# One quarter of x transposed by TensorE and three quarters by DMA, rows of Q padding and output weights loaded elsewhere, and the plan drawn from 24 candidates

## The chip, the cores and the metric

The kernel runs on one core of a Trainium2 chip. The metric is device time in microseconds (us). The kernel before took 361.9 us, the median of three runs (361.76 to 362.11). A difference below 0.2% (0.7 us) cannot be told from no change here.

## The reference: what is computed

One block of multi-head attention with S = 2048 rows, model width D = 448, 16 heads of 28 columns each, all in bf16:

```python
qkv = (x @ wqkv).reshape(B, S, 3, H, Dh)          # x: 1 x 2048 x 448, wqkv: 448 x 1344
q, k, v = ...                                     # each B, H, S, Dh
scores = jnp.einsum("bhqd,bhkd->bhqk", q, k) * (Dh ** -0.5)
p = _softmax(scores, axis=-1)
o = jnp.einsum("bhqk,bhkd->bhqd", p, v)
out = o.transpose(0, 2, 1, 3).reshape(B, S, D) @ wo
```

## The kernel before, in words

**Tiling.** Heads are taken in 4 groups of 4 (G, HG), each head padded from 28 to 32 rows, so that a group fills 128 partitions. The queries are cut into 4 chunks of 512 (QW, NQC), the keys into 16 blocks of 128 (NKT). One pair of group and chunk is a *set*; there are 16 sets. Within a set every head has 16 steps, one for each block of keys: a score matmul of 128 keys by 512 queries (line 730), the exponential, and a matmul of the result with V that adds into the set's accumulator `o` (line 1073). That makes 1024 steps in all.

**Two paths for the exponential.** ScalarE takes two steps at once: one `activation` with Exp over 128x1024 values of PSUM tile `a0` or `a1` into `pt` (line 928). VectorE takes single steps: it turns the scores of PSUM bank `d0`, `d1` or `m` into int16 bit patterns `I` that read as bf16 powers of two (line 943), and adds two shifted copies `J` (line 1014); for some chains one copy is made by GpSimd's fill (line 979) and an accumulating DMA (line 990). 358 instructions of ScalarE take 716 steps and 308 of VectorE the other 308.

**What comes first.** Before the first scores can be computed, the kernel needs:

- x with its columns on the partitions (`XT`, four blocks b of 512 rows). x arrives in `xs[b]` as eight loads of half a block, four from SP's DMA queue and four from ScalarE's (lines 145 to 149). TensorE transposes each block against an identity, two banks of eight transposes for each block (`xt_job`, line 621); ScalarE copies one bank to `XT` (line 629) and VectorE the other (line 627). The contraction of 448 is cut into 4 pieces of CK = 112.
- the weights of group 0 for K and Q (`WG`, loads of 232-byte rows, lines 151 and 152), and later all three weights (`WRAW`, line 136).
- K of all four blocks for group 0 (`k_first`, projections at line 298), its squares on ScalarE (`sq`, line 324), column sums by TensorE (line 409), their maximum on VectorE (`kp`, line 414) and a root: the softmax's bound is the product of a query's norm and the largest norm of a key. This bound rides along as extra rows of Q.
- Q of set 0 (`z`, line 457) and its bound (`su`, line 496).

**Q's padding rows.** For each chunk c, half k and buffer z there is a tile `QP[c][k][z]`. VectorE clears all 16 of them (line 194), then SP issues 16 small DMAs of a constant `offs` into some of their rows (line 198), then four DMAs bring set 0's rows of `z` into them (`rows_first`, line 661), then two bring `su` (line 502). Until these have landed, a score of set 0 is made of two matmuls, with `z` and with `su`; afterwards of one, with `QP` (`emit_s`, line 730). The text below calls the first form *narrow*.

```python
terms = [QP[c][i % 2][g % 2]] if w else [qtt[0], held["su0"]]
```

**GpSimd's opening** clears the V tiles (lines 209, 210) and the output weights `WO` (line 216), and issues 16 DMAs that load `WO` head by head (line 219).

**Order of the work.** `tc.manual_schedule()` is on: every engine runs its instructions in the order in which the program emits them. The middle of the program is a planner. It keeps a clock for each engine (`free`), a table of events with the time at which it believes them to happen (`evt`), and PSUM banks with the time at which they come free (`res`); a job (`add`) has an engine, an assumed duration, the events it needs and a priority. The planner moves the engine with the earliest clock, picks what that engine does next (`pick_pe`, `pick_act`, `pick_dve`, `pick_pool`, `pick_sp`), and emits it. Its times only set the order: on the chip each instruction waits for its real inputs. Loads are given to it as fixed due times:

```python
for n, t in (("x", 0), 4.9), (("G", 1), 6.9), (("G", 0), 6.9), (("x", 1), 6.2), (("x", 2), 8.0), (("x", 3), 9.3), \
        (("W", 2), 10.9), (("W", 0), 12.0), (("W", 1), 13.2):
    evt[n] = (t, "DMA")
```

**End of a set.** VectorE copies `o` to `o_sb` (line 1100); SP gathers the denominators, scatters their reciprocals to DRAM and spreads them (lines 1105, 1114, 1120); GpSimd multiplies (line 1123) into `xs` or `OTL`. Output projections (`oproj_job`) and stores (line 600) follow once all four groups of a chunk are done; the last chunk has a hand-written end (lines 1293 to 1350).

Of the kernel before, what the change touches and what calls it, by code (L numbers as in the profile page):

```python
# [16 lines left out]
LAT = 0.2  # L17
# [20 lines left out]

@with_exitstack
def kernel(  # L40
# [16 lines left out]
    CK = D // CC  # L57
# [11 lines left out]
    NXB = NKT // XB  # L69
    SHIFT = (0, 43, 85)  # L70
# [20 lines left out]
    NSET = G * NQC  # L91
    GH = 2
# [6 lines left out]
    out_perm = out2.rearrange("(p t) d -> p t d", t=NKT)  # L99
# [7 lines left out]
    XT = [[big.tile([CK, CC // 2, QW], BF16, name=f"XT{b}_{k}") for k in range(2)] for b in range(NXB)]  # L107
# [15 lines left out]
    xs = [big.tile([P, XB, D], BF16, name=f"xs{b}") for b in range(NXB)]  # L123
    QP = [[[big.tile([P, QW], BF16, name=f"QP{c}_{k}_{z}") for z in range(2)] for k in range(2)] for c in range(NQC)]
    OTL = [big.tile([P, QW], BF16, name=f"OTL{c}") for c in range(NQC)]

    def otile(g, c):
        if g < G - 1:
            return xs[c][:].rearrange("p t d -> p (t d)")[:, g * QW:(g + 1) * QW]
        return OTL[c][:]  # L130

    wq3 = wqkv.rearrange("(cc p) n -> p cc n", p=CK)
    x3 = x2.rearrange("(p t) c -> p t c", t=NKT)

    def load_w(t, eng):
        eng.dma_start(out=WRAW[t][:, :, 0:D], in_=wq3[:, :, t * D:(t + 1) * D])

    def load_x(b, eng, k=0, n=1):
        w = XB // n
        eng.dma_start(out=xs[b][:, k * w:(k + 1) * w, :], in_=x3[:, b * XB + k * w:b * XB + (k + 1) * w, :])  # L140

    def load_w0(t, eng):
        eng.dma_start(out=WG[t], in_=wq3[:, :, t * D:t * D + HG * Dh + WPAD])
# [33 lines left out]
    offs = wk.tile([P, 2 * QW], BF16, name="pt", bufs=NPT)[0:2, 0:QW]  # L177
# [12 lines left out]
    nc.vector.memset(offs, OFFS)  # L190
    for c in range(NQC):
        for k in range(2):
            for z in range(2):
                nc.vector.memset(QP[c][k][z][:], 0.0)
    for z in range(2):
        for c in range(NQC):
            for k in range(2):
                nc.sync.dma_start(out=QP[c][k][z][HP * k + Dh + NQC - 1 - c:P:2 * HP, :], in_=offs)
# [4 lines left out]
    for t in range(3):  # L203
        nc.gpsimd.memset(WRAW[t][:, :, D:D + WPAD], 0.0)

# [21 lines left out]
    def pair_tile(tg):  # L227
        return psum.tile([P, 2 * QW], F32, name=tg, tag=tg, bufs=1)

    def bank_tile(tg):  # L230
        return psum.tile([P, QW], F32, name=tg, tag=tg, bufs=1)


    free = {"PE": 0.0, "ACT": 0.0, "DVE": 0.0, "SP": 0.0, "POOL": 26.0}
    port = {"DVE": 0.0, "POOL": 0.0}
    evt = {}
    res = {"a0": 0.0, "a1": 0.0, "d0": 0.0, "d1": 0.0, "o": 0.0, "m": 0.0}
    ops = {"PE": [], "ACT": [], "DVE": [], "SP": [], "POOL": []}
    cnt = {"step": 0, "half": 0}
    held = {}  # L240
    cur = {"c_end": 0.0, "s": 0, "u": 0, "o": None, "oset": 0, "pv": 0, "half": 0, "o_open": False}
    parts = {}

    def add(eng, dur, emit, **k):
        op = Op(eng, dur, emit, **k)
        ops[eng].append(op)
        return op

    def ready(op):
        if cnt["step"] < op.gate or (op.acq == "m" and op.gives[0][0] == "O" and left() < OLAST):  # L250
            return None
        if op.acq == "m" and op.pri > 5 and ("KN0", NQC - 1) not in evt:
            return None
        r = 0.0
        for n in op.need:
            if n not in evt:
                return None
            t, e = evt[n]
            r = max(r, t + (0.03 if e == op.eng else LATS.get((e, op.eng), LAT)))
        if op.acq is not None:  # L260
            if res[op.acq] is None:
                return None
            r = max(r, res[op.acq])
        return r + op.lag

    def run(op, t):
        op.emit()
        if op.eng == "PE":
            note(t, op.cols)
        end = t + op.dur  # L270
        if op.eng == "PE" and main_on():
            cur["c_end"] = end
        if op.port:
            port[op.eng] = end
        for n in op.gives:
            evt[n] = (end + op.land, op.eng)
        if op.after is not None:
            op.after(end)
        if op.acq is not None:
            res[op.acq] = None  # L280
        if isinstance(op.rel, tuple):
            parts.setdefault(op.rel[0], []).append(end + LATS.get((op.eng, "PE"), LAT))
            if len(parts[op.rel[0]]) == op.rel[1]:
                res[op.rel[0]] = max(parts.pop(op.rel[0]))
        elif op.rel is not None:
            res[op.rel] = end + LATS.get((op.eng, "PE"), LAT)
        ops[op.eng].remove(op)
        return end


    KAt, QAt, sqt, kst, kmt = {}, {}, {}, {}, {}

    def mm_proj(ps, t, g, c, ccs):
        for cc in ccs:
            for i in range(HG):
                h = g * HG + i
                w = WG[t] if g == 0 else WRAW[t]
                nc.tensor.matmul(out=ps[HP * i:HP * (i + 1), :], lhsT=w[:, cc, h * Dh:h * Dh + HP],  # L298
                                 rhs=XT[c][cc // 2][:, cc % 2, :], start=(cc == 0), stop=(cc == CC - 1),
                                 tile_position=(0, HP * i))  # L300

    def quarters(out, lhsT, rhs, start, stop, **k):
        for i in range(P // HP):
            r = slice(HP * i, HP * (i + 1))
            nc.tensor.matmul(out=out[r, :], lhsT=lhsT[:, r], rhs=rhs, start=start, stop=stop, tile_position=(0, HP * i), **k)  # L305

    def after_shared(m):

        if "shared" in cur:
            tc.add_manual_dep(m.ins, cur["shared"].ins.name,  # L310
                              mybir.DependencyInfo(mybir.DependencyClass.Sync, mybir.DependencyReason.DATA),
                              reason="GpSimd's pass stays behind VectorE's")

    def new_sq(key):
        sqt[key] = wk.tile([P, QW], BF16, name="sq", tag="sq", bufs=4)
        return sqt[key]

    def square(key, src):
        t = new_sq(key)
        after_shared(nc.gpsimd.tensor_tensor(out=t[:], in0=src, in1=src, op=ALU.mult))  # L320

    def act_square(key, mask):
        t = new_sq(key)
        nc.scalar.activation(out=t[:], in_=held[key][:, 0:QW], func=ACT.Square, scale=mask[:, 0:1])

    def k_job(g, sc, bank, pri, gate=0, split=2):
        key = ("K", g, sc)
        n = CC // split

        def mm(part):  # L330
            if part == 0:
                held[key] = bank_tile(bank) if bank[0] != "a" else pair_tile(bank)
            mm_proj(held[key][:, 0:QW], 1, g, sc, range(part * n, (part + 1) * n))

        def evac():
            KAt[(g, sc)] = big.tile([P, QW], BF16, name=f"KA{sc}", tag=f"KA{sc}", bufs=2)
            src = held[key][:, 0:QW]
            nc.vector.tensor_scalar(out=KAt[(g, sc)][:], in0=src, scalar1=kmask[:, 0:1],  # L338
                                    scalar2=ones[:, 0:1], op0=ALU.mult, op1=ALU.add)

        for p in range(split):
            add("PE", n * D_WAVE, lambda p=p: mm(p), pri=pri, gate=gate, cols=448 * n,
                need=[("XT", sc, 0), ("XT", sc, 1), ("W", 1)] + ([key + (p - 1,)] if p else []), gives=[key + (p,)],
                acq=bank if p == 0 else None)
        add("DVE", 0.72, evac, need=[key + (split - 1,)], gives=[key], rel=bank, pri=pri)
        add("POOL", 1.08, lambda: square(key, KAt[(g, sc)][:]), need=[key], gives=[("ksq", g, sc)], pri=pri, port=True)

    def kn_job(g, bank, pri, gate=0):
        key = ("KN", g)

        def mm(sc):
            if sc == 0:
                held[key] = bank_tile(bank) if bank[0] != "a" else pair_tile(bank)
            quarters(held[key][:, 0:QW], maskK[:, sc, :], sqt.pop(("K", g, sc))[:], sc == 0, sc == NQC - 1)
# [1026 lines left out]
```

## Time and profile before

| what | value |
| --- | --- |
| median of three runs | 361.9 us |
| the profiled execution's own time | 361.72 us |
| its span | 359.9 us |
| PE, ScalarE, VectorE, GpSimd busy | 343.1, 341.1, 335.4, 170.2 us |
| the exponentials (line 928): count, busy | 358, 329.7 us |
| first exponential starts, last one ends | 19.39 us, 351.27 us |
| granted TensorE clock | 0.998 |

The span runs from the first to the last instruction that the profile shows; the profiled execution took 1.82 us more than its span. Times of single instructions are counted from the span's start. "PE" is TensorE; a queue's name with a small q (SPq) stands for the issue of DMAs. The chain of waits goes back from the last instruction to whatever released it, so it shows which work set the end; a group of instructions with much busy time that is not in the chain costs nothing.

### The profile page before, as it was taken

The numbers are of one execution on the slowest core, as the hardware profiler recorded it, in microseconds if no ns is written. First come the engines' busy times: TensorE is split into PE (matmuls) and PEld (weight loads), VectorE is DVE, ScalarE is ACT, GpSimd is POOL, SyncE is SP. The second block draws the span as 40 slices with busy tenths as digits, with TensorE's granted clock in tenths as the row PEclk, the third lists the DMA queues.
The fourth block names the chain that finished last, engine by engine and source line by source line (L and its number), as shares of the span: only waits on it lengthen the run. The fifth ranks groups of instructions, "written<-read, shape, count | busy, mean of one in ns | idle before, by whom it ended". The sixth has DMA issues, their size and how long they took to land.

```text
span 359.9 us, 11256 instructions
## 1 busy us (share of the span) xinstructions
PE 343.1 (95%) x4520; PEld 111.3 (31%) x4521; DVE 335.4 (93%) x617; ACT 341.1 (95%) x373; POOL 170.2 (47%) x213
## 2 busy tenths in 40 slices
PE   8999999999999999999999999999889999999995
PEld 4533233332234322332232222222222222222233
DVE  8689999999989999999899999999999999999863
ACT  3789999999999999999999999999999999999991
POOL 8951353655444483545635765465546362521010
PEclk9999999999999999999999999999999999999999
DMA  8620063555636765365577646377857685672111
GB/s 242 142 47 15 21 125 86 113 107 105 135 75 129 148 124 113 89 132 108 117 143 149 120 91 137 78 152 158 177 116 156 128 176 129 142 147 66 34 51 54
DMA packets 24017, 41.17 MB, mean 114 GB/s; under 512 B 8604, under 2 KB 15004, under 8 KB 23964
## 3 DMA queue, kind: packets, MB, share of 16 engines
q0 software_dynamic: 8432, 29.24, 42.0%
q1 hardware_dynamic: 14348, 10.07, 10.3%
q10 hardware_dynamic: 1184, 1.14, 1.0%
q8 instruction: 35, 0.57, 0.6%
q14 instruction: 18, 0.15, 0.1%
HBM read 7.58 MB, written 1.96 MB: 27 GB/s over the span
## 4 chain that ended last, share of the span: by engine, by line
PE 37%; ACT 30%; DVE 23%; issue 9%; DMA 1%; DVEq 0%; ACTq 0%
ACT pt L928 30%; PE a L730 12%; DVE I L943 10%; PE o L1073 10%; PE m L305 5%; DVE J L1014 5%; PE m L298 4%; DVE V L579 2%; DVE V L566 2%; DVE KA L338 1%; PE o L643 1%; PE d L730 1%; DVE QA L460 1%; DVE o_sb L1100 1%; PE d L621 1%
## 5 line engine op out<-in xcount | busy, mean ns | idle before, releaser
L928 ACT ACTIVATE pt<-a 128x1024 bf16<-128x1024 f32 x358 | 329.7, 1129 | 2.9 <-PE a L730 1.3
L943 DVE TENSOR_SCALAR I<-d 128x512 int16<-128x512 f32 x278 | 181.0, 680 | 10.1 <-PE d L730 8.8
L730 PE MATMUL a<-QP,KA 32*128 32x512 bf16 (+1 forms) x704 | 137.3, 381 | 8.9 <-ACT pt L928 8.0
L1073 PE MATMUL o<-pt,V 128*32 128x512 bf16 x716 | 105.2, 384 | 0.0
L730 PE MATMUL d<-QP,KA 32*128 32x512 bf16 (+1 forms) x273 | 95.7, 383 | 0.8 <-DVE I L943 0.2
L730 PEld LDWEIGHTS <-KA 32*128 32x128 bf16 (+1 forms) x1041 | 46.1, 91 | 143.5 <-issue 141.7
L990 POOL DMA_DIRECT2D J<-I x55 | 49.6, 902 | 73.0 <-DVE I L943 49.6
L1073 PE MATMUL o<-J,V 128*32 128x512 bf16 x616 | 82.7, 384 | 0.0
L979 POOL MEMSET J<- 128x1024 int32 x55 | 60.1, 1094 | 36.7 <-PE d L730 12.0
L1014 DVE TENSOR_SCALAR J<-I 128x2048 int16<-128x2048 int16 x99 | 73.9, 764 | 0.6
L1073 PE MATMUL o<-I,V 128*32 128x512 bf16 x308 | 64.3, 384 | 0.1
L1073 PEld LDWEIGHTS <-V 128*32 128x32 bf16 x1640 | 30.8, 94 | 48.2 <-issue 45.1
L1123 POOL TENSOR_TENSOR xs<-o_sb,rr 128x512 bf16<-128x512 f32 x12 | 16.9, 1404 | 27.3 <-DVE J L1014 26.9
L298 PE MATMUL m<-XT,WRAW 112*32 112x512 bf16 x384 | 29.6, 384 | 0.2 <-DVE QA L460 0.2
L320 POOL TENSOR_TENSOR sq<-QA 128x512 bf16<-128x512 bf16 x15 | 16.8, 1122 | 23.1 <-DVE QA L460 17.8
L305 PE MATMUL m<-WRAW,XT 112*32 112x112 bf16 (+1 forms) x768 | 20.7, 230 | 0.3 <-DVE KA L338 0.3
L943 DVE TENSOR_SCALAR I<-m 128x512 int16<-128x512 f32 x30 | 20.3, 678 | 0.0
L320 POOL TENSOR_TENSOR sq<-KA 128x512 bf16<-128x512 bf16 x12 | 14.2, 1185 | 9.4 <-DVE J L1014 8.5
L305 PEld LDWEIGHTS <-XT 112*32 112x32 bf16 x768 | 12.3, 96 | 11.5 <-issue 11.4
L305 PE MATMUL m<-WO,xs 128*32 128x448 bf16 x156 | 12.5, 358 | 0.0
L730 PE MATMUL m<-QP,KA 32*128 32x512 bf16 (+1 forms) x30 | 11.5, 384 | 0.0
L460 DVE CAST QA<-m 128x512 bf16<-128x512 f32 x15 | 10.2, 683 | 0.7 <-PE m L298 0.7
(116 smaller groups left out, 207.3 us busy)
## 6 DMA issues: line engine op xcount, KB each, us to landing
J<-I POOLq DMA_DIRECT2D x55, 512.0 KB, 4.9
rr<-scr SPq DMA_DIRECT2D x60, 64.0 KB
QP<-QA SPq DMA_DIRECT2D x60, 28.0 KB
out_dram<-osb SPq DMA_DIRECT2D x12, 112.0 KB
WRAW<-in_wqkv_dram SPq DMA_DIRECT2D x3, 392.0 KB
xs<-in_x_dram ACTq DMA_DIRECT2D x4, 224.0 KB
xs<-in_x_dram SPq DMA_DIRECT2D x4, 224.0 KB
QP<-su SPq DMA_DIRECT2D x32, 2.0 KB
```

The lines of the kernel that those rows point to most:

```text
L298: nc.tensor.matmul(out=ps[HP * i:HP * (i + 1), :], lhsT=w[:, cc, h * Dh:h * Dh + HP], rhs=XT[c][cc // 2][:, cc % 2, :], start=(cc == 0), s ...
L305: nc.tensor.matmul(out=out[r, :], lhsT=lhsT[:, r], rhs=rhs, start=start, stop=stop, tile_position=(0, HP * i), **k)
L320: after_shared(nc.gpsimd.tensor_tensor(out=t[:], in0=src, in1=src, op=ALU.mult))
L460: nc.vector.tensor_copy(out=t[:], in_=held[key][:, 0:QW])
L730: nc.tensor.matmul(out=out_ap, lhsT=KAt[(g, j // XB)][r, (j % XB) * P:(j % XB + 1) * P], rhs=q[r, :], start=(n == 0), stop=(n == len(terms ...
L928: nc.scalar.activation(out=pt[:], in_=ps[:], func=ACT.Exp, scale=LN2 / 128.0)
L943: nc.vector.tensor_scalar(out=dst, in0=pd[:], scalar1=BIAS, scalar2=0.0, op0=ALU.add, op1=ALU.max)
L979: m = nc.gpsimd.memset(ch[1][:].bitcast(I32), fill)
L990: after_shared(nc.gpsimd.dma_start(out=ch[1][:, w], in_=ch["I"][:, w], accum_op=ALU.add))
L1014: cur["shared"] = nc.vector.tensor_scalar(out=r[:, w], in0=ch["I"][:, w], scalar1=float(SHIFT[k]), scalar2=None, op0=ALU.add)
L1073: nc.tensor.matmul(out=o[HP * i:HP * (i + 1), :], lhsT=VT[e["k"]][g, j // XB][:, j % XB, HP * i:HP * (i + 1)], rhs=e["ap"], start=(SETMM[k ...
L1123: m = nc.gpsimd.tensor_tensor(out=otile(g, c), in0=st["o_sb"][:], in1=st["rr"][:], op=ALU.mult)
```

## The change

- **x.** Of the four blocks of x only block 0 (`NPL = 1`) is still loaded as rows and transposed by TensorE, as 16 transposes of 128x128. Blocks 1 to 3 come by four transposing DMAs on SP's queue: one, `XE`, brings columns 320 to 447 of all 1536 rows, three bring columns 0 to 383 of 512 rows each. The pieces of the contraction become CK = 128 rows; the fourth overlaps the third by 64 rows, for which the weights are zeroed. `xt(b, cc)` finds a piece. As x is now tiled by blocks of rows, the output's row order changes with it (`out_at`).
- **Weights.** Each load is two DMAs (three pieces of 128 rows and one of 64). Group 0's weights come on ScalarE's queue, `WRAW[2]` after the transposes on SP's, and `WRAW[0]`, `WRAW[1]` become planner jobs behind set 0's bound. VectorE and GpSimd zero the 64 rows.
- **Q's padding.** VectorE still clears all 16 tiles, in another order; `offs` is set by GpSimd in a tile of its own. Two of the 16 small DMAs stay on SP, 14 go to GpSimd's queue.
- **Output weights.** `WO` is cleared and loaded by planner jobs on GpSimd and SP after Q of chunk 3 of group 0, no longer in GpSimd's opening.
- **Plan.** The planner is a function `plan`, run 24 times without emitting anything, with small random changes (`shake`) of two of its thresholds for all but seed 0; the seed that ends first by the planner's clock is then emitted. The due times and some banks and priorities of the opening are other ones.

The diff's core, without the change of indentation:

```diff
-    CK = D // CC
+    CK = P
+    CT = D - CK
+    NPL = 1
+    NSEED = 24
...
-    XT = [[big.tile([CK, CC // 2, QW], BF16, name=f"XT{b}_{k}") for k in range(2)] for b in range(NXB)]
+    XT = [[big.tile([CK, CC // 2, QW], BF16, name=f"XA{b}_{k}") for k in range(2)] for b in range(NPL)]
+    XT += [big.tile([CK, CC - 1, QW], BF16, name=f"XT{b}") for b in range(NPL, NXB)]
+    XE = big.tile([CK, 1, S - NPL * QW], BF16, name="XE")
...
+    def xt(b, cc):
+        if b < NPL:
+            return XT[b][cc // 2][:, cc % 2, :]
+        return XT[b][:, cc, :] if cc < CC - 1 else XE[:, 0, (b - NPL) * QW:(b - NPL + 1) * QW]
...
+    def load_w(t, eng, n=D):
+        dst = WG[t] if n < D else WRAW[t][:, :, 0:D]
+        cols = slice(t * D, t * D + n)
+        eng.dma_start(out=dst[:, 0:CC - 1, :], in_=wqkv[0:(CC - 1) * CK, cols].rearrange("(cc p) n -> p cc n", p=CK))
+        eng.dma_start(out=dst[CC * CK - D:CK, CC - 1, :], in_=wqkv[(CC - 1) * CK:D, cols])
+    def load_x(b):
+        rows = slice(b * QW, (b + 1) * QW)
+        nc.sync.dma_start_transpose(out=XT[b][:], in_=x2[rows, 0:(CC - 1) * CK])
...
-    load_x(0, nc.sync, 0, 2)
-    load_x(0, nc.scalar, 1, 2)
-    for b in range(1, NXB):
-        load_x(b, nc.sync, 0, 2)
-        load_x(b, nc.scalar, 1, 2)
-        if b == 1:
-            load_w0(1, nc.sync)
-            load_w0(0, nc.scalar)
+    for b in range(NPL):
+        for eng, k in ((nc.sync, 0), (nc.scalar, 1)):
+            t = slice(k * XB // 2, (k + 1) * XB // 2)
+            eng.dma_start(out=xp[b][:, t, :], in_=x2[b * QW:(b + 1) * QW].rearrange("(p t) c -> p t c", t=XB)[:, t, :])
+    for t in range(2):
+        nc.vector.memset(WG[t][0:CC * CK - D, CC - 1, :], 0.0)
+    for t in (1, 0):
+        load_w(t, nc.scalar, HG * Dh + WPAD)
+    nc.sync.dma_start_transpose(out=XE[:], in_=x2[NPL * QW:S, CT:D])
+    for b in range(NPL, NXB):
+        load_x(b)
     load_w(2, nc.sync)
-    load_w(0, nc.sync)
-    load_w(1, nc.sync)
...
-                nc.sync.dma_start(out=QP[c][k][z][HP * k + Dh + NQC - 1 - c:P:2 * HP, :], in_=offs)
+    nc.gpsimd.memset(offs[:], OFFS)
+    offs_rows(0, 0, nc.sync)
...
+        nc.gpsimd.memset(WRAW[t][0:CC * CK - D, CC - 1, 0:D], 0.0)
...
-    for gg in range(G):
-        nc.gpsimd.memset(WO[:, gg, :], 0.0)
-    for h in range(H):
-        g, i = divmod(h, HG)
-        nc.gpsimd.dma_start(out=WO[HP * i:HP * i + Dh, g, :], in_=wo[h * Dh:(h + 1) * Dh, :])
+    for c in range(1, NQC):
+        offs_rows(c, 0, nc.gpsimd)
+    for c in range(NQC):
+        offs_rows(c, 1, nc.gpsimd)
...
+        def shake(w):
+            return rnd.uniform(-w, w) if seed else 0.0
...
-    for n, t in (("x", 0), 4.9), (("G", 1), 6.9), (("G", 0), 6.9), (("x", 1), 6.2), (("x", 2), 8.0), (("x", 3), 9.3), \
-            (("W", 2), 10.9), (("W", 0), 12.0), (("W", 1), 13.2):
+        for n, t in [(("x", 0), 4.9), (("x", 1), 99.0)] + [(("XT", k, h), 8.9 + 1.8 * (k - NPL)) for k in range(NPL, NXB) for h in range(2)] + \
+                [(("G", 1), 6.7), (("G", 0), 6.7), (("W", 2), 14.2)]:
         evt[n] = (t, "DMA")
...
-            evt[("QZ", c, z)] = (6.5, "DVE")
+                evt[("QZ", c, z)] = (9.5 if c + z == 0 else 20.0 if z == 0 else 24.0, "DMA")
...
+        for gg in range(G):
+            add("POOL", 0.5, lambda gg=gg: clear_wo(gg), need=[("QA", 0, CL)], gives=[("WZ", gg)], pri=95, port=True)
+        for h in range(H):
+            add("SP", 0.55, lambda h=h: load_wo(h), need=[("WZ", h // HG)], gives=[("WO", h)], pri=9, land=2.5)
...
-    k_first(0, "a0", None, "DVE", "ACT", 1.5)
-    k_first(1, "a1", "o", "ACT", "ACT", 3.05, late=("ksq", 0, NQC - 1))
-    k_first(2, "d0", "a0", "ACT", "ACT", 3.1, late=("ksq", 0, NQC - 1))
-    k_first(3, "d1", "o", "DVE", "ACT", 3.2, late=("QA", 0, 0))
+        k_first(0, "a0", "o", "DVE", "ACT", 1.5)
+        k_first(1, "a1", "a0", "ACT", "ACT", 3.05, late=("ksq", 0, NQC - 1))
+        k_first(2, "d0", "o", "ACT", "ACT", 3.1, late=("ksq", 0, NQC - 1))
+        k_first(3, "d1", "a0", "DVE", "ACT", 3.2, late=("QA", 0, 0))
...
+        for t in range(2):
+            add("SP", 1.2, lambda t=t: load_w(t, nc.sync), need=["QP00"], gives=[("W", t)], land=6.0, pri=3)
...
-        return fin <= free["ACT"] + D_EXP * (len(exps) + max(0, left() // 2 - 2)) + 0.2
+            return fin <= free["ACT"] + D_EXP * (len(exps) + max(0, left() // 2 - 2)) + 0.2 + shake(0.4)
...
-        if can_add and t > adds[0][0]["at"] + AGE:
+            if can_add and t > adds[0][0]["at"] + AGE + shake(1.0):
...
+    d = Dry()
+    ends = {k: plan(d, d, d, d, d, d, k, True) for k in range(NSEED)}
+    seed = min(ends, key=lambda k: ends[k])
+    plan(nc, tc, psum, big, wk, dram, seed, False)
```

More of the change, by code (lines that the diff above doesn't have):

```diff
@@ L1 @@
+import random
 from contextlib import ExitStack
@@ L266, in run @@
[L266 to L288, printed above, removed]
@@ L291 @@
[L291 to L305, printed above, removed]
@@ L307, in after_shared @@
[L307 to L346, printed above, removed]
@@ new lines, in plan @@
+        for t in range(2):
+            add("SP", 1.2, lambda t=t: load_w(t, nc.sync), need=["QP00"], gives=[("W", t)], land=6.0, pri=3)
+        add("SP", 2.4, rows_first, need=[("Q", 0, 0), ("QZ", 0, 0)], gives=["QR00"], land=1.6, pri=0)
+        for b in range(NXB):
+            v_job(0, b, 0, "m", 7 + 4 * b, eng="ACT" if b == 0 else "DVE")
+            vs_job(0, b, 7 + 4 * b + 3)
+        q_job(0, 1, "m", 16.2)
+        qn_job(0, [1], "m", 16.21)
+        for c in range(2, NQC):
+            q_job(0, c, "m", 30 + c)
@@ new lines, in far_chain, with emit, accumulate, landed @@
+        def far_chain(ch):
+            n = len(chain["all"])
+            fill = SHIFT[1] * 65537
+            def emit():
+                m = nc.gpsimd.memset(ch[1][:].bitcast(I32), fill)
+                after_shared(m)
+            ch["id"] = n
+            add("POOL", 1.05, emit, gives=[("fill", n)], pri=20, port=True)
+        def accumulate(ch, m):
+            w = slice(0, m * QW)
+            ch["acc"] = None
+            def emit():
+                after_shared(nc.gpsimd.dma_start(out=ch[1][:, w], in_=ch["I"][:, w], accum_op=ALU.add))
+            def landed(end):
+                at = ch["acc"] = end + ACC_LAND
+                for n in range(m):
+                    pending.append({"step": ch["steps"][n], "k": 1, "ap": ch[1][:, n * QW:(n + 1) * QW].bitcast(BF16),
+                                    "ready": at, "pt": None, "ch": ch})
+            evt[("I4", ch["id"])] = (free["DVE"], "DVE")
+            add("POOL", 0.88, emit, need=[("fill", ch["id"]), ("I4", ch["id"])], gives=[("acc", ch["id"])], pri=10, port=True)
+            ops["POOL"][-1].after = landed
@@ new lines, in best @@
+        def best(eng, t):
+            b, nxt = None, None
+            for op in ops[eng]:
+                r = ready(op)
+                if r is None:
+                    continue
+                if op.port:
+                    r = max(r, port["POOL" if eng == "DVE" else "DVE"])
+                if r <= t:
+                    if b is None or op.pri < b.pri:
+                        b = op
+                elif nxt is None or r < nxt:
+                    nxt = r
+            return b, nxt
@@ new lines, in nmin, with urgent @@
+        def nmin(*v):
+            v = [x for x in v if x is not None]
+            return min(v) if v else None
+        def urgent(op):
+            n = op.gives[0]
+            if op.more:
+                return True
+            if n[0] not in ("K", "KNp", "Q", "QN", "V") or n[1] == 0:
+                return False
+            g = GH if n[1] is None else n[1]
+            first = min(k for k in range(NSET) if ORDER[k][0] == g)
+            if n[0] == "V":
+                return sum(len(q) for k in range(first) for q in remain[k]) < URGENT_V
+            return sum(len(q) for k in range(first) for q in remain[k]) < URGENT
```

1835 lines of the change are left out of this document (928 added, 907 removed).

## The prediction, made before the changed kernel ran

> **What bounds the kernel.** I read the page's first part, then the chain of waits, then the timelines of ScalarE, TensorE and SP's queue in the opening.
>
> ```profile
> span 359.9 us, 11256 instructions
> PE 343.1 (95%) x4520; PEld 111.3 (31%) x4521; DVE 335.4 (93%) x617; ACT 341.1 (95%) x373; POOL 170.2 (47%) x213
> ...
> L928 ACT ACTIVATE pt<-a 128x1024 bf16<-128x1024 f32 x358 | 329.7, 1129 | 2.9 <-PE a L730 1.3
> ```
>
> Three engines are 93 to 95% busy, so the stages have to be parted. The 358 exponentials run from 19.39 to 351.27 us. In undisturbed stretches of the chain they start 0.905 us apart (six steps from 171.52 to 176.95). Back to back they need 357 x 0.905 + 1.02 = 324.1 us and take 331.9: 7.8 us of slip. So time = opening (19.4) + exponentials (324.1) + slip (7.8) + end (8.6). The instruction order of the changed kernel has again 358 exponentials, 308 `I` (276 + 32, before 278 + 30) and the same end: the second and fourth terms stay; opening and slip are open.
>
> The chain of waits in the opening (start, us, what):
>
> ```profile
> 5.64 1.49 PE d L621 x16
> 7.13 0.45 PE o L621 x8
> 7.57 0.45 PE m L621 x8
> 8.02 0.98 PE a L298 x16
> 9.00 1.03 PE d L621 x16
> ...
> 11.01 0.58 PE o L621 x8
> ...
> 14.85 1.01 PE d L298 x16
> 15.90 0.04 issue
> 15.94 0.70 ACT sq L324
> ```
>
> From 5.64 to 15.86 TensorE works without a pause, and a third of it is transposes (L621). Then one chain runs to the first exponential: last K projection done, square, column sum, maximum, root, `su`, scores: 19.39 - 15.86 = 3.5 us. The opening is thus set by when K of block 3 can start, now 14.85.
>
> ScalarE next, then SP's queue:
>
> ```profile
> 19.39 1.94 ACT L928 ACTIVATE pt<-a 128x1024 bf16<-128x1024 f32 x2 [0.68 <-PE a L730]
> 21.51 1.94 ACT L928 ACTIVATE pt<-a 128x1024 bf16<-128x1024 f32 x2 [0.19 <-PE d L730]
> 23.67 1.02 ACT L928 ACTIVATE pt<-a 128x1024 bf16<-128x1024 f32 x1 [0.22 <-PE d L730]
> 24.95 7.44 ACT L928 ACTIVATE pt<-a 128x1024 bf16<-128x1024 f32 x8 [0.25 <-PE d L730]
> ```
> ```profile
> 7.63 11.51 SPq L198 DMA_DIRECT2D QP<-pt  x16
> 19.24 3.22 SPq L661 DMA_DIRECT2D QP<-z  x4
> 22.56 1.09 SPq L502 DMA_DIRECT2D QP<-su  x2
> ```
>
> Five exponentials take 24.95 - 19.39 = 5.56 us instead of 4.53: narrow scores cost 1.0 us. They last until SP has issued all of `QP`, at 23.65; the first scores from `QP` start at 25.15, 1.5 us later. What holds SP is its 16 small DMAs, 0.72 us each.
>
> **The change, part by part.**
>
> *TensorE.* Gone are the transposes of blocks 1 to 3: 0.90 + 1.03 + 1.03 us. Block 1's hid the copies that K of block 0 waits for, and that wait (7.13 to 8.02) stays. The new order is K0, Q0, K1, sum, filler, K2, two sums, K3. VectorE's first memsets are two more (0.11 each, as `blockK`'s), which move the warm-up and all behind it by 0.2. So K3 can start at 8.2 + 4 x 0.98 + 0.2 + 0.2 + 2 x 0.32 = 13.2 instead of 14.85, if x is there. Pieces of 128 instead of 112 rows cost nothing: matmuls of 32, 112 and 128 rows by 512 take 381, 384 and 384 ns (L730, L298, L1073). ScalarE and VectorE lose three copies each (1.0 and 0.67 us).
>
> *Transposing DMAs.* The trace has none. 4 x 393 KB follow block 0 on SP's queue. Nearest rows are plain loads: 380 GB/s for rows of 1792 bytes (3 to 4 us), 240 to 250 for pieces of 896 bytes (10 to 13 us), and by the packet records 203 KB of 232-byte rows in 1.4 us, 145 GB/s.
>
> ```profile
> 3.00:4.00 1.00, 1.00 (x4) 0.32 (x3) 0.99 (x5) 0.00 (x0) 0.92 (x4) 1.00 1.03 384
> 10.00:11.00 1.00, 1.00 (x18) 0.36 (x18) 1.00 (x2) 0.64 (x1) 0.94 (x3) 1.00 1.13 238
> ```
>
> (The last column is GB/s.) Block 0 is in by 3.9, group 0's weights take 1.4 us: 5.3. `XE` reads pieces of 256 bytes, nearest to 232: 2.7 us. The three `XT` read 768 bytes, nearest to 896: 1.6 each. Sum 12.8. For completion I take 1.0 (block 0's last packet is at 3.9, its transposes start at 5.43: at most 1.5). K3 starts at 13.8: **1.05 us gained**; bounds are 1.65 gained (all at 380, TensorE bounds) and 2.25 lost (all at 145: 5.3 + 10.8 + 1.0 = 17.1). `WRAW[2]` comes 1.6 us behind the last transpose, at 15.4, and is needed behind K3's sum, at about 15.9; later, the scores queued behind V on TensorE wait with it.
>
> The Trainium skill ("DMA: Bandwidth & Descriptors", Latency and other measured facts) gives transposing DMAs 261 GB/s with a non-contiguous middle dimension; by that the four take 6.0 us (an estimate), K3 is bound by TensorE and the gain is 1.65 instead of 1.05. The 238 GB/s above are near it.
>
> *Narrow scores.* SP's 16 DMAs become 2. In SP's order now: transposes (taken to hold SP until about 12.5), two loads 1.0, two small DMAs 1.4, four of `z` 3.2, two of `su` 1.1: 19.2, and with 1.5 to landing 20.7. `z` itself is ready near 12, so SP sets this. The instruction order has 4 narrow exponentials instead of 6. From 18.35 the fifth needs its scores near 21.5, so 0.8 us cover a late `QP`; beyond it ScalarE stands as long as `QP` is late. Gain between 0 and 0.6: I take **0.4**, two fifths of 1.0.
>
> *At nothing.* GpSimd: -8.5 (16 `WO` DMAs) - 1.8 (its clears) + 14 x 0.53 + 0.5 + 3 x 0.5; it ends near 22 as now (23.0); its next work, and chunk 1's rows on SP, start at 30. `WO` on SP later: 16 DMAs of at most 0.83 us = 13 us ahead of set 0's denominators. Now GpSimd multiplies set 0 at 66.5; 79.5 still precedes set 2's copy to `o_sb` (two buffers; copies at 44.6 and 66.3, the next near 88). Without that cover `o` stays occupied and ScalarE loses the excess. Clearing `WO` takes 2 us in GpSimd's gaps of 3 to 5. Full Q and K weights, behind `su`, land near 25; K of group 1 is first evacuated at 46.4. Store order: same bytes.
>
> *Schedule.* Of the slip 6.8 us lie behind the narrow stretch, in gaps of 0.1 to 0.5. The best of 24 by the planner's clock may lose fewer or, as that clock is not the chip, more. Bounds: 1.5 either way, five gaps of 0.3. I take one and a half gaps fewer: **0.5**.
>
> **Sum.** 1.05 + 0.4 + 0.5 = 1.95. Own time 361.72 - 1.95 = 359.8; this execution lies 0.2 below the median 361.9, so I forecast **359.9**, own range 358.2 (all best: 1.65 + 0.6 + 1.5) to 361.1.
>
> **Rivals.**
>
> *The transposes arrive late* (slower). Place: K3's start. It decides where the last block is ready after 14.85 + 0.4 = 15.25, or 14.25 without completion: 1573 KB in 8.95 us, 176 GB/s. Below it each us late costs a us. At 145 GB/s: 2.25 - 0.4 = 1.85 slower, 363.8; at 100, 21.0 + 1.0 = 22.0: 6.75 slower, 368.7. [...] Against: 768-byte pieces in three of four. Chance 0.16.
>
> *The new schedule slips more* by 1.5 to 2 us, which eats the opening's 1.45: 362 to 362.4, ScalarE gaps in mid-kernel. For: 7.8 us of slip show how far the plan's clock is from the chip; against: same work, same totals. Chance 0.13.
>
> *Blocks of 128x128 pass one after another*, each at the price of a DMA alone. The nearest row is `WO`'s 24.5 KB, 2.0 us from issue to landing: 48 x 2.0 = 96, K3 at 102.3, 87 us slower: 449. Against: those 16 were issued 0.53 us apart, so landings overlap. Chance 0.03. The Trainium skill ("VectorE: DVE Perf Modes", The three transpose paths) speaks against this change: 1309 ns for such a block by DMA against 390 by TensorE; by that 63 us and 416 (an estimate). TensorE's here are 0.45 us for eight, so its column is a latency, which pipelining hides; whether the DMA's is too no run here shows yet.
>
> *Nothing gained*: K3 gets x in time but waits elsewhere (`WRAW[2]`, `QP`), 361.5 to 362. Chance 0.06. The forecast keeps 0.62.
>
> **Chances.** Below 361.2 (faster by over 0.2%, what a measurement can tell from no change): forecast 0.61, late x 0.02, schedule 0.03: 0.66. Within 0.2%: 0.01 + 0.02 + 0.07 + 0.04 = 0.14. Slower: 0.12 + 0.03 + 0.03 + 0.02 = 0.20. The range 358.2 to 363.8 reaches to 145 GB/s and leaves out worse transposes and little else.
>
> **What would show it.** TensorE: K3's projection at 13.2 to 13.8 (line 335). First exponential near 18.3, fifth from wide scores, without a gap over 0.3 before it. SP: `z` issued by 18. Last exponential's end minus first's start 331.0. Wrong: a pause of TensorE before K1 or K3 that ends with a DMA, or equal opening and another slip.

## The result and the profile after

The changed kernel takes 360.98 us, the median of 16 runs (359.73 to 361.64), the kernel before 361.67 (16 runs). The ratio is 0.9976, with a 95% interval of 0.9966 to 0.9986: 0.9 us faster (0.5 to 1.2), just past what counts as a difference here. The forecast was 1.95 us.

The page of the changed kernel, its first lines and the group of exponentials:

```profile
span 359.1 us, 11135 instructions
...
PE 336.9 (94%) x4453; PEld 108.3 (30%) x4454; DVE 333.8 (93%) x615; ACT 339.1 (94%) x370; POOL 174.3 (49%) x215
...
L978 ACT ACTIVATE pt<-a 128x1024 bf16<-128x1024 f32 x358 | 330.5, 1121 | 3.5 <-PE a L780 1.6
```

The same 358 exponentials, the span 0.8 us shorter. ScalarE's timeline in the opening:

```profile
16.91 1.94 ACT L978 ACTIVATE pt<-a 128x1024 bf16<-128x1024 f32 x2 [0.78 <-PE a L780]
19.04 11.34 ACT L978 ACTIVATE pt<-a 128x1024 bf16<-128x1024 f32 x12 [0.19 <-PE d L780]
```

The first exponential starts at 16.91 instead of 19.39, and the narrow stretch has one break in place of three. Split like the prediction's sum (all from the two profiled executions):

| term | before | after | change | forecast |
| --- | --- | --- | --- | --- |
| first exponential starts | 19.39 | 16.91 | -2.48 | -1.05 |
| slip of the first six intervals (narrow) | 1.05 | 0.60 | -0.45 | -0.4 |
| slip of the rest | 6.72 | 8.57 | +1.85 | -0.5 |
| behind the last exponential | 8.65 | 8.88 | +0.23 | 0 |
| span | 359.9 | 359.1 | -0.8 | -1.95 |

Of the 1.85, 0.22 is the last exponential's own time (1.25 us, before 1.03); the rest lies between the starts. So the opening and the narrow stretch gave 2.9 us, twice what was forecast, and two of them were lost again behind it. (Some 0.4 of the 2.48 belongs to these two executions, as the experiment on contraction rows shows.) The chain of waits in the opening (start, us, what):

```profile
5.76 1.01 PE d L661 x16
...
7.43 1.05 PE a L335 x16
8.48 0.86 PE m L335 x16
9.34 0.86 PE a L335 x16
...
10.80 1.05 PE d L335 x16
...
12.90 0.61 DVE V L528
...
13.98 1.35 DVE kp L451 x2
```

K0, Q0 and K1 follow each other without transposes between them, and from K2 on the chain goes through VectorE's maxima, no longer through K3. K3's projection runs from 12.31; the forecast had 13.8. Behind it little has changed: the first exponential follows K3's start by 4.60 us, before by 4.54. SP's queue and the stretches of the DMA (the last column is GB/s):

```profile
1.19 1.47 SPq L182 DMA_TRANSPOSE XE<-in_x_dram  x1
2.71 6.15 SPq L171 DMA_TRANSPOSE XT<-in_x_dram  x3
...
10.26 1.22 SPq L226 DMA_DIRECT2D QP<-offs  x2
11.57 3.78 SPq L709 DMA_DIRECT2D QP<-z  x4
```
```profile
4.00:5.00 1.00, 1.00 (x4) 0.31 (x3) 0.99 (x5) 0.79 (x1) 0.94 (x4) 1.00 1.27 287
...
8.00:9.00 1.00, 1.00 (x28) 0.54 (x20) 0.00 (x0) 0.47 (x1) 0.94 (x4) 1.00 1.20 247
9.00:10.00 1.00, 1.00 (x24) 0.42 (x16) 0.75 (x1) 0.82 (x2) 0.94 (x3) 1.00 0.97 133
```

The four transposes are packets of 256 bytes in the trace, from 3.7 to 11.1 us; with group 0's weights, which run beside them until 6.8, they make 230 to 290 GB/s, with a dip at 9 to 10. They hold SP until 8.86, and `z` goes out from 11.57, where the forecast had up to 18: the fifth exponential finds its scores in time.

### The profile page after: what moved, and what is told of

The parts are those of the page before. It is cut to its first block, busy times and chain, and to the rows that moved or that the text cites. A ratio compares the mean times of both kernels' runs of the same rounds, so it can differ in the third digit from the quotient of the medians.

```text
span 359.1 us, 11135 instructions
## 1 busy us (share of the span) xinstructions
PE 336.9 (94%) x4453; PEld 108.3 (30%) x4454; DVE 333.8 (93%) x615; ACT 339.1 (94%) x370; POOL 174.3 (49%) x215
## 3 DMA queue, kind: packets, MB, share of 16 engines
q1 hardware_dynamic: 20516, 11.22, 12.2%
## 4 chain that ended last, share of the span: by engine, by line
PE 41%; ACT 32%; DVE 11%; issue 8%; DMA 6%; POOL 1%; SPq 0%; DVEq 0%; POOLq 0%; ACTq 0%
ACT pt L978 32%; PE a L780 14%; PE o L1123 11%; PE m L342 5%; DVE I L993 5%; PE m L335 4%; DMA J<-I 4%; DVE J L1064 2%; DMA rr<-scr 2%; PE o L679 1%; DMA scr<-rec 1%; PE d L780 1%; DVE KA L375 1%; DVE kp L451 1%; PE a L335 1%
## 5 line engine op out<-in xcount | busy, mean ns | idle before, releaser
L780 PE MATMUL a<-QP,KA 32*128 32x512 bf16 (+1 forms) x708 | 138.1, 381 | 11.1 <-ACT pt L978 9.8
L1123 PE MATMUL o<-pt,V 128*32 128x512 bf16 x716 | 108.2, 383 | 0.0
L780 PE MATMUL d<-QP,KA 32*128 32x512 bf16 (+1 forms) x273 | 98.5, 383 | 0.2
L1123 PE MATMUL o<-J,V 128*32 128x512 bf16 x616 | 87.2, 384 | 0.9 <-DVE J L1064 0.4
L1029 POOL MEMSET J<- 128x1024 int32 x55 | 58.4, 1061 | 48.4 <-PE d L780 13.5
L1040 POOL DMA_DIRECT2D J<-I x55 | 52.7, 957 | 58.1 <-DVE I L993 50.2
L1123 PE MATMUL o<-I,V 128*32 128x512 bf16 x308 | 68.2, 383 | 0.7 <-DVE o_sb L1150 0.6
L993 DVE TENSOR_SCALAR I<-m 128x512 int16<-128x512 f32 x32 | 21.8, 680 | 0.2 <-PE m L780 0.2
L335 PE MATMUL m<-XT,WRAW 128*32 128x512 bf16 x216 | 18.3, 386 | 0.1
L342 PE MATMUL m<-WRAW,XT 128*32 128x112 bf16 (+1 forms) x432 | 13.7, 231 | 0.2
L342 PE MATMUL m<-sq,maskK 128*32 128x512 bf16 x108 | 10.8, 389 | 1.4 <-POOL sq L357 1.2
```

Source lines behind the costliest of these rows:

```text
L780: nc.tensor.matmul(out=out_ap, lhsT=KAt[(g, j // XB)][r, (j % XB) * P:(j % XB + 1) * P], rhs=q[r, :], start=(n == 0), stop=(n == len(terms ...
L993: nc.vector.tensor_scalar(out=dst, in0=pd[:], scalar1=BIAS, scalar2=0.0, op0=ALU.add, op1=ALU.max)
L1029: m = nc.gpsimd.memset(ch[1][:].bitcast(I32), fill)
L1040: after_shared(nc.gpsimd.dma_start(out=ch[1][:, w], in_=ch["I"][:, w], accum_op=ALU.add))
L1123: nc.tensor.matmul(out=o[HP * i:HP * (i + 1), :], lhsT=VT[e["k"]][g, j // XB][:, j % XB, HP * i:HP * (i + 1)], rhs=e["ap"], start=(SETMM[k ...
```

## The experiments

Two theories for the 1.85 us. **D, the draw:** the slip belongs to the order of instructions that was emitted; a new opening makes the planner emit another order, and the candidate that its own clock puts first need not be best on the chip. **M, moved work:** the loads and clears of `WO`, now in mid-kernel, cost it. A third, **C**: the planner's clock says nothing about candidates.

### Other candidates of the same plan

Edit, for seeds 0, 15, 18, 9 and 19; opening and work are the same, but seeds 0 and 15 use 360 exponentials instead of 358:

```diff
-    ends = {k: plan(d, d, d, d, d, d, k, True) for k in range(NSEED)}
-    seed = min(ends, key=lambda k: ends[k])
+    seed = 0
```

> The changed kernel with the unshaken plan (seed 0) in place of the drawn one (seed 14). By the planner's own clock it ends at 347.3 us, the drawn one at 345.6, the kernel before at 347.2. Opening as in the changed kernel: first exponential at 16.9 us. Theory D (slip belongs to the order of instructions that is emitted, and the planner's clock ranks orders roughly): slip between first and last exponential grows from 9.0 us by about 1.7, time 1 to 2 us above the changed kernel, near 362.5. Rival M (slip comes from the work that the change moved into mid-kernel, the loads and clears of WO): slip stays near 9.0, time within 0.4 us of the changed kernel. Rival C (the planner's clock says nothing): either sign.

> The changed kernel with the candidate that the planner's clock puts last of the 24 (seed 15, 348.7 us against 345.6 for the drawn one). First exponential at 16.9 us. Theory D: slip 3 us larger than 9.0, time near 364. Rival M: within 0.4 us of the changed kernel. Rival C: either sign.

> The changed kernel with the second candidate of the planner's clock (seed 18, 345.8 us). First exponential at 16.9 us. Theory D with the clock as a rough guide: within 0.7 us of the changed kernel. Rival M: within 0.4 us too. Rival C: anything from 359.5 to 363.

> The changed kernel with the third candidate of the planner's clock (seed 9, 346.1 us). So far the clock's 345.6, 345.8, 347.3 and 348.7 us went with 360.9, 358.9, 361.0 and 361.5 on the chip. If the clock is a rough guide: 359.0 to 360.6. If it is none within 1 us: anything from 358.9 to 361.5, and the time follows the span from the first to the last exponential, not the opening (16.5 to 17.5).

> As before with seed 19 (346.3 us by the planner's clock). If the clock is a rough guide: 359.2 to 360.8. If it is none within 1 us: anything from 358.9 to 361.5.

Measured, with the changed kernel (seed 14) on top. "First to last" runs from the start of the first exponential to the end of the last; the slip is what the intervals between the exponentials' starts have beyond 0.905 us each:

| seed | planner's clock | time | ratio to before (95%) | first exponential | first to last | exponentials | slip |
| --- | --- | --- | --- | --- | --- | --- | --- |
| 14 | 345.6 | 360.98 | 0.9976 (0.9966 to 0.9986) | 16.9 | 333.3 | 358 | 9.0 |
| 18 | 345.8 | 358.87 | 0.9932 (0.9919 to 0.9945) | 16.9 | 330.7 | 358 | 6.4 |
| 9 | 346.1 | 359.56 | 0.9933 (0.9911 to 0.9956) | 17.3 | 331.6 | 358 | 7.3 |
| 19 | 346.3 | 360.02 | 0.9952 (0.9934 to 0.9970) | 17.3 | 332.8 | 358 | 8.5 |
| 0 | 347.3 | 361.01 | 0.9984 (0.9975 to 0.9994) | 17.2 | 333.6 | 360 | 7.6 |
| 15 | 348.7 | 361.45 | 0.9989 (0.9976 to 1.0003) | 16.5 | 333.6 | 360 | 7.5 |

M is refuted as the main cause. With the same moved work, the same start of the first exponential and as many exponentials, seed 18 slips 2.6 us less than the drawn order, and less than the kernel before (7.8). Seeds 0 and 15 are slow for another reason: their two more exponentials cost 1.8 us (2 x 0.905), while their slip is smaller than the drawn order's.

The numbers that were expected of D for the first three missed all the same. Seed 18 is 2.1 us better than the changed kernel (1.6 by the ratios), not within 0.7 of it. Seeds 0 and 15, which were to slip more and be 1 to 2 and 3 us worse, slip less and are 0 and 0.5 worse; by its time alone seed 0 would fit M. Seeds 9 and 19 fall into both of their ranges and part nothing.

The five that were not drawn come in the clock's order, with time minus clock between 12.8 and 13.7 us, though neighbours' intervals overlap and the last two are the ones with 360 exponentials. The drawn one has 15.4: it is the one that the clock flatters most. As far as six orders can tell, C falls too: the clock is a guide over 3 us, not over one.

### The changed kernel again

No edit.

> The changed kernel once more, on the same chip as the others of this set: 361.0 us, 0.9976 of the kernel before; first exponential at 16.9 us; the spread between profiles shows how much of the slip repeats with the same order.

360.87 us, ratio 0.9981 (0.9972 to 0.9990); first exponential at 16.52, span 358.2. The slip of each 24 intervals between exponentials, from their starts in the trace (us beyond 0.905 each; the first column holds the narrow stretch):

```
before          1.22 0.13 0.78 0.29 0.35 0.80 1.05 0.28 0.11 0.61 0.25 0.83 0.12 0.56 0.37
changed         0.86 0.55 0.52 1.13 0.25 0.08 0.63 0.55 1.33 0.42 1.73 0.14 0.25 0.40 0.12
changed again   0.87 0.55 0.52 1.09 0.25 0.07 0.63 0.39 1.27 0.42 1.31 0.14 0.23 0.41 0.12
no WO           0.90 0.15 0.50 0.94 0.24 0.08 0.63 0.39 1.19 0.42 1.32 0.14 0.23 0.41 0.12
no WO again     0.87 0.15 0.49 1.04 0.24 0.09 0.62 0.40 1.22 0.41 2.09 0.14 0.23 0.41 0.11
seed 18         0.85 0.16 0.87 0.40 0.15 0.23 1.01 0.33 0.25 0.54 0.22 0.72 0.08 0.30 0.25
```

"No WO" is the next experiment; it has the drawn order too. The same order repeats its pattern to about 0.05 us in most columns; the 4th, 8th, 9th and 11th vary by 0.14 to 0.8 us. Three columns (4th, 9th, 11th) hold most of the loss, and they are other columns in other orders. This is D's fingerprint. What such a loss looks like, in the changed kernel's timelines of TensorE, GpSimd and ScalarE:

```profile
96.41 0.38 PE L780 MATMUL d<-QP,KA 32*128 32x512 bf16 x1
97.59 0.40 PE L342 MATMUL m<-sq,maskK 128*32 128x512 bf16 x4 [0.79 <-POOL sq L357]
```
```profile
83.71 1.29 POOL L1173 TENSOR_TENSOR xs<-o_sb,rr 128x512 bf16<-128x512 f32 x1 [5.34 <-DMA rr<-scr]
...
95.59 0.87 POOL L1040 DMA_DIRECT2D J<-I  x1 [2.03 <-DVE I L993]
96.20 1.34 POOL L357 TENSOR_TENSOR sq<-QA 128x512 bf16<-128x512 bf16 x1
```
```profile
98.63 1.02 ACT L978 ACTIVATE pt<-a 128x1024 bf16<-128x1024 f32 x1 [0.44 <-PE d L780]
```

A column sum for a later bound stands ahead of scores on TensorE and waits for a square on GpSimd; the next scores start late, and ScalarE stands. GpSimd starts this square at 96.20, right behind the issue of a `J`, for which it had waited 2.03 us for VectorE's `I`. Its longer wait, 5.34 us for set 1's denominators, ended at 83.71, before a smaller gap at 87 us (0.37), and is not the cause of this one: in the next experiment GpSimd multiplies set 1 at 82.58, and the gap at 97 stays. A planner that counts on shorter latencies than the chip's would queue work in this way; no run here tried it with other latencies.

TensorE has other such waits in the drawn order: for VectorE's `QA` at 152 (0.65 us), for its `J` at 258.6 (0.43), for the accumulating DMA's `J` at 243.9 (0.35). The last one is what varies in the 11th column: it took 0.35 us where the column has 1.73, 0.70 where it has 2.09, and was absent where it has 1.31 and 1.32.

### Without the moved loads of WO

```diff
+    for gg in range(G):
+        nc.gpsimd.memset(WO[:, gg, :], 0.0)
...
-            add("POOL", 0.5, lambda gg=gg: clear_wo(gg), ...
+            add("POOL", 0.5, lambda gg=gg: None, ...
-            add("SP", 0.55, lambda h=h: load_wo(h), ...
+            add("SP", 0.55, lambda h=h: None, ...
```

The order of everything else is the drawn one.

> The changed kernel in its own order, but without the mid-kernel work on the output weights: GpSimd clears WO in the opening, and the 16 loads of WO are left out, so the output projections multiply by zeros. Opening unchanged. Rival M: the gaps of ScalarE at 86 and 97 us (0.37 and 0.68 us, which go back to GpSimd waiting for the late denominators of set 1) vanish, time 0.8 to 1.2 us below the changed kernel. Theory D: these gaps come from set 1's own scatter and spread and stay, time within 0.4 us of the changed kernel.

> The kernel without mid-kernel work on the output weights once more (its loads are left out, GpSimd clears WO in the opening), since its first result, 360.2 us and 0.9967 (0.9954 to 0.9980), doesn't part 0 from 0.8 us. Theory D: 360.4 to 361.0, 0.9967 to 0.9983. Rival M: 359.6 to 360.2, under 0.9962.

360.21 us and 0.9967 (0.9954 to 0.9980), then 360.45 and 0.9964 (0.9950 to 0.9979), against 0.9976 and 0.9981 with the loads: some 0.45 us better, with intervals that overlap, and between the two expectations or at their edges. The profile is sharper: in the table only the second column changes by more than it varies between profiles of one kernel, from 0.55 to 0.15, so the moved loads cost **0.4 us** in this order. The gap at 97 us stays, and TensorE's timeline of the kernel without them names the same releaser:

```profile
97.36 0.40 PE L344 MATMUL m<-sq,maskK 128*32 128x512 bf16 x4 [0.78 <-POOL sq L359]
```

Orders 18, 9, 19, 0 and 15, which have the loads, lose only 0.05 to 0.16 in that column: even this cost is one of the order.

### The kernel before in other orders

The kernel before with the change's `shake` in its two thresholds (0.4 and 1.0 us), nothing else:

```diff
-        return fin <= ... + 0.2
+        return fin <= ... + 0.2 + shake(0.4)
-        if can_add and t > adds[0][0]["at"] + AGE:
+        if can_add and t > adds[0][0]["at"] + AGE + shake(1.0):
```

> The kernel before with nothing changed but its schedule: the two thresholds shaken as in the change, and the best of 24 by the planner's clock taken (seed 15, 346.8 us; unshaken 347.2). Opening unchanged, first exponential at 19.4 us. Theory D (slip belongs to the order that is emitted): time between first and last exponential differs from 331.9 us by up to 2 us either way. If the planner's clock is a guide: 361.2, 0.5 us below the kernel before. Rival: any order of this planner loses the same, within 0.3 us of the kernel before.

> The kernel before, its two thresholds shaken with seed 11: a middling candidate of its 24 (349.0 us by the planner's clock, the middle of the 24 is 348.6; unshaken 347.2). Theory D, that the kernel before owes part of its time to a good order: 362.5 to 363.5, one to two us above the kernel before. Rival, that orders of this planner differ by less than a run's spread: 361.2 to 362.0.

Seed 15, the clock's best of 24: 362.16 us, 1.0017 (1.0008 to 1.0025), so 0.6 us slower where the clock promised 0.4 faster; its slip is 8.7 us for 7.8. Seed 11, a middling one: 363.75, 1.0056 (1.0035 to 1.0076), 2 us slower, a little more than D expected. It has 360 exponentials, and the two more account for 1.8 of the 2 us; its slip is 8.9. The plan of the kernel before is thus better than both of its own other candidates that ran: it lies 8th of 24 by its clock (346.8 to 350.7) and did better still on the chip. And again the clock's first choice has the largest time minus clock: 15.4, against 14.4 unshaken and 14.7 for seed 11. Choosing among 24 did for the old opening what it did for the new one: the choice by the clock alone gave nothing.

### One transposing DMA more

```diff
+    load_x(NXB - 1)
     nc.sync.dma_start_transpose(out=XE[:], in_=x2[NPL * QW:S, CT:D])
```

> The changed kernel in its own order, with one transposing DMA more (block 3, 393 KB) ahead of the four; it is overwritten by the later one. All four then land about 1.5 us later (256-byte packets at 250 to 285 GB/s). Theory T (the opening is bound by TensorE, and x has slack): K of block 1 at 9.15 us has 0.5 to 1.5 us of slack; first exponential 0 to 1 us later. Rival X (the transposes bind): first exponential 1.5 us later, time 1.5 us more.

363.91 us, 1.0060 (1.0047 to 1.0072): 3.0 us more than the changed kernel; first exponential at 19.55. TensorE's timeline of this kernel, K of blocks 1, 2 and 3:

```profile
10.62 0.83 PE L336 MATMUL a<-XT,o_sb 128*32 128x512 bf16 x12 [1.12 <-DMA XT<-in_x_dram]
12.49 0.83 PE L336 MATMUL d<-XT,o_sb 128*32 128x512 bf16 x12 [0.51 <-DMA XT<-in_x_dram]
14.96 0.83 PE L336 MATMUL d<-XT,o_sb 128*32 128x512 bf16 x12 [0.88 <-DMA XT<-in_x_dram]
```

Now every K waits for its block. The trace records a DMA's completion as 16 steps of a semaphore; the last step for blocks 1, 2 and 3 comes at 10.57, 12.45 and 14.91 us, and the three K start within 0.05 us of it. In the changed kernel's profile it comes at 8.08, 10.09 and 11.58, and K1, K2 and K3 start later, at 9.15, 10.80 and 12.31, K3 without any idle time ahead of it:

```profile
12.31 0.83 PE L335 MATMUL d<-XT,o_sb 128*32 128x512 bf16 x12
```

So one transpose more delays the blocks by 2.4 to 3.3 us, not by the 1.5 that was expected, and the K by 1.47, 1.69 and 2.65. The differences, 1.0, 0.7 and 0.7 us, are the slack that x had. Theory T's mechanism is right for the changed kernel's profile: x is ready, and TensorE binds the opening. Its number, 0 to 1 us for the first exponential, missed, and rival X's 1.5 came nearer only because the added transpose costs more than was expected. Beyond the slack the prediction's rule holds, a us for a us: K3 starts 2.65 us later and the first exponential 2.64. The slack is small, though. In the ten profiles with four transposes K3 has 0 to 1.2 us of it, and with seed 9, where K0 starts earliest (6.55), K2 and K3 do wait for x.

### Contraction rows

```diff
-                nc.tensor.matmul(... lhsT=w[:, cc, h * Dh:h * Dh + HP], rhs=xt(c, cc), ...
+                nc.tensor.matmul(... lhsT=w[0:112, cc, h * Dh:h * Dh + HP], rhs=xt(c, cc)[0:112], ...
```

and the same in V's projection.

> The changed kernel in its own order, with every projection of x contracting only rows 0 to 111 of each piece of 128; the other 16 rows of a piece are left out of the sums. The transposing DMAs and all else stay. In the profile of the changed kernel 16 such matmuls take 0.86 us of TensorE's time, before 0.98. Theory R (the number of contraction rows sets it): with 112 rows they take 0.98 again, the first exponential comes 0.4 to 0.6 us later than at 16.9, and the time grows by that or a little more. Rival (the pace comes from something else in the opening, the source of the transposed data or the neighbours): 0.86 stays, same time as the changed kernel.

TensorE's timeline of this kernel, K0, Q0 and K1:

```profile
8.03 1.05 PE L335 MATMUL a<-XA,o_sb 112*32 112x512 bf16 x16
8.90 1.04 PE L335 MATMUL m<-XA,rr 112*32 112x512 bf16 x16
9.77 0.82 PE L335 MATMUL a<-XT,o_sb 112*32 112x512 bf16 x12
```

With 112 rows the next group still starts 0.87 us later: R is refuted, rows cost nothing, as the prediction said. The 0.98 of the kernel before comes from what follows: there a group of 16 is followed by transposes or by a column sum over all 128 columns of the array. In the changed kernel K1 too takes 0.99 (9.15 to 10.14) ahead of such a sum, and K0 and Q0 take 0.86 ahead of their own kind. The Trainium skill ("TensorEngine Tiling (Array Packing)", Key Properties) says that a change of tiling mode drains TensorE; the trace agrees, at 0.12 us a change.

The time, 361.02 us and 0.9988 (0.9976 to 1.0001), is that of the changed kernel again within the noise (360.87). The first exponential, 17.51, is later because K0 started later already, at 8.03 against 7.43. In nine of the ten profiles with four transposes the first exponential follows K0's start by 9.5 to 9.6 us (by 10.8 with seed 9, where x is late), and in all ten it follows K3's by 4.60. What moves K0 is the time that block 0's 16 transposes take. TensorE's timelines, first of the kernel before, then of the changed kernel, the changed kernel again and this kernel:

```profile
5.43 1.69 PE L621 MATMUL d<-ident,xs 128*112 128x128 bf16 x16
```
```profile
5.56 1.22 PE L661 MATMUL d<-ident,xs 128*128 128x128 bf16 x16
```
```profile
5.31 1.06 PE L661 MATMUL d<-ident,xs 128*128 128x128 bf16 x16
```
```profile
5.56 1.89 PE L661 MATMUL d<-ident,xs 128*128 128x128 bf16 x16
```

Single transposes start 0.11 us apart before some moment of each execution and 0.06 apart after it. The trace's record of TensorE's granted clock begins at the same moment: at 6.8, 5.9, 5.0 and 7.3 us in these four. Block 0's loads are complete by 4.4 us in all ten profiles, before its transposes start, so they are not what varies. What sets the moment no run here shows.

This bears on the opening's gain, since the kernel before was caught with a late moment. Its first exponential came at 19.39 with 1.69 us for the 16 transposes, and in its order of seed 11 at 19.02 with 1.25. At a like pace the new opening has 17.2 to 17.3 (seeds 0 and 19, 1.60 and 1.70 us) and 16.9 (the changed kernel and seed 18, 1.22 and 1.20). So the change itself is worth about 2.1 us there (an estimate from these pairs); some 0.4 of the 2.48 is the luck of two executions.

## Why the prediction was right and wrong

**The step that failed** is "Schedule": "I take one and a half gaps fewer: 0.5". In place of 0.5 us gained the drawn order lost 1.85 in the profiled execution and 1.16 in the second; from the first exponential's start to the last one's end it took 333.3 us, where 331.0 was to show that the forecast was right. The rival that named it ("the new schedule slips more by 1.5 to 2 us", chance 0.13) happened. Its bound of 1.5 either way was too tight: nine orders of this planner ran, and the six with the same opening lie 2.6 us apart (2.1 by the ratios). The reason against it, "same work, same totals", carried little weight: seed 18 does the same work with 2.6 us less slip. That the kernel still came out 0.9 us faster, and not at that rival's 362 to 362.4, is luck: the opening was undervalued, and the two errors partly cancel. I also gave no thought to the fact that the least of 24 by a rough clock is likely the one in which the clock errs most.

**Opening, right in mechanism, too small in size**: 2.48 us (2.87 in the second profile, about 2.1 at a like pace of TensorE) for 1.05. K3's start sets the first exponential as the prediction said: it came 2.54 us sooner (12.31 for 14.85), the exponential 2.48. The sum had x bind K3; TensorE did.
- Transposes: arrival for K3 was put at 13.8. The last block was complete at 11.58, 0.7 us before K3 ran. The rows that I called nearest were too slow: with group 0's weights beside them the 256-byte packets made 230 to 290 GB/s in most stretches. The 145 of the 232-byte rows was not their limit, since in the same 1.4 us (4.7 to 6.1) x's packets of 1792 bytes moved another 135 GB/s. The Trainium skill's 261 GB/s ("DMA: Bandwidth & Descriptors", Latency and other measured facts), which I weighed and left aside, was nearer, though the mean from 3.7 to 11.1 us, weights beside them, is 1573 KB / 7.4 us = 213.
- TensorE: bound of 13.2 was 0.9 too late. K0 and Q0 take 0.86 each ahead of their own kind (0.24), and K0 started at 7.43, not 8.2: block 0's transposes were done sooner, in part because TensorE's pace doubled at 5.9 us instead of 6.8, and the 0.2 for two more memsets came to 0.13 (the warm-up starts at 1.32, before at 1.19).
- What is late next: VectorE's maxima, which I had not named; from 12.2 on they are the chain, though level with K3's own path, as the 4.60 us from K3 to the first exponential show.

**Narrow scores**: 0.45 for 0.4, right. `z` was issued from 11.57 and no stall came before the fifth exponential.

**At nothing**: right for GpSimd's opening, Q's padding and the late weights, all of which end before their next use. Not for `WO`: 0.4 us in this order.

**The other rivals**: late transposes would have cost a us for a us beyond their slack, but were in time in the profile of the changed kernel. Blocks one after another are excluded: 48 blocks in 7.4 us are 0.15 us each. The 1309 ns of the Trainium skill ("VectorE: DVE Perf Modes", The three transpose paths) are, if anything, the latency of one; no run here measures one alone.

**A version that beats both**: seed 18, 358.87 us, 0.9932 (0.9919 to 0.9945). The by-engine line of the chain of waits, first of the changed kernel, then of seed 18:

```profile
PE 41%; ACT 32%; DVE 11%; issue 8%; DMA 6%; POOL 1%; SPq 0%; DVEq 0%; POOLq 0%; ACTq 0%
```
```profile
ACT 50%; PE 35%; issue 9%; DVE 4%; DVEq 0%; ACTq 0%
```

With seed 18 the chain is ScalarE's exponentials for half of the span and no DMA is in it. In its profile it keeps the 2.9 us of the opening and the narrow stretch and adds 0.7 saved behind them.

**Open**: why the planner's clock flatters the drawn orders. That its latencies are short for the scatter of denominators and the accumulating DMA would fit the gap at 87 us and the wait at 243.9; planning with longer ones was not tried. Open too: what sets the moment at which TensorE's pace doubles.

## What to carry to other kernels

Where a planner or a random draw sets the order, any change elsewhere redraws it, and the redraw can be worth more than the change: split the measured difference into opening, steady part and end, and run a few orders of both versions before crediting the change. Choose among candidates by running the best few on the chip, since the first by an imperfect clock is the one that its errors favour. A transfer that replaces compute in an opening is priced from its own packets' rate and from what is late next, and both sides deserve a look at their slack: by the times at which the transfers are complete, and by adding one transfer more. Openings of single executions are compared only where TensorE reached its full pace at a like moment.

## What was not expected of the hardware

- Sixteen packed matmuls of 512 columns take 0.86 us ahead of their own kind and 0.98 ahead of matmuls over the whole array, with 112 as with 128 contraction rows.
- A transposing DMA of 393 KB holds SP's queue for 1.5 to 2.5 us (1.47 for `XE`, 6.15 for three `XT`), so what stands behind it on SP is issued only as the transposes drain, while the issue of the plain loads around them takes 0.4 to 0.6.
- The same order of instructions repeats its losses to about 0.05 us in most stretches. The largest variation from run to run, 1.31 to 2.09 us in the 11th column of one order, goes with a wait for one DMA (none to 0.70 us).
- TensorE's pace doubled at 4.1 to 7.3 us in the profiles with the changed kernel's opening, although the warm-up starts at 1.32 in all of them; this moves the first exponential by up to 1 us from execution to execution.
